# Attention gradients on one core: the query-major exponentials 384 wide with a quarter taken by DMA transposes, and the gradient score matmuls of a half-step on both sides of its burst

## The chip, the core and the metric

The kernel runs on one core of a Trainium2 chip. Time is device time in microseconds (us), from runs of the whole program. One execution was also taken by the hardware profiler; the profile names the engines PE (TensorE matmuls), PEld (TensorE weight loads), DVE (VectorE), ACT (ScalarE), POOL (GpSimd) and SP (SyncE, which only issues DMAs here). The granted TensorE clock (PEclk) is given in shares of full speed.

## The reference

Two branches over the same input are mixed by a gate, and the program returns the output and the gradients of twelve inputs. Cut to what matters here:

```python
x = A_x                                            # 1 x 2048 x 576, bfloat16
g = sigmoid((x * gate_w).sum(-1, keepdims=True))
# branch A: attention, 32 heads of 18
q, k, v = split(x @ wqkv)
p = softmax(einsum("bhqd,bhkd->bhqk", q, k) * 18 ** -0.5)
a = einsum("bhqk,bhkd->bhqd", p, v) ... @ wo
# branch B: a long convolution whose kernel is a sum of complex exponentials
P = exp(logdA[:, :, None] * l)                     # 576 x 128 x 2048
K = einsum("dn,dnl,dn->dl", Cc, P, dB).real
b = irfft(rfft(x) * rfft(K)) + x * Dskip
out = g * a + (1 - g) * b
grads = vjp(out, grad_out)    # of x, wqkv, wo, the seven parameters of B, gate_w
```

The change lies in the gradient of branch A: for every head, the 2048 x 2048 exponentials, dV = P^T dO, dP = dO V^T, dS = P * dP, and dQ, dK from dS.

## The kernel before

The program has three stretches: projections (to about 125 us), the attention loop with its gradients (to about 2105 us), and the convolution branch with the last weight gradients (to the end).

**The attention loop.** Heads go in 8 groups of 4; a *unit* is one group with one block of 512 queries (32 units). The keys come in 16 tiles of 128. Each unit's forward pass is 32 *half-steps*, each for one key tile and one pair of heads; its gradient pass takes 32 half-steps too and runs `OFF` = 39 half-steps behind, so that in nearly every iteration of `for G in range(...)` (L1289) a forward half-step of one unit and a gradient half-step of the unit before it stand side by side. The schedule is written out by hand: instructions go to each engine's queue in program order. One iteration, in PE's order:

- `P1`: two score matmuls K·Q^T, keys on the partitions, one head each, into a PSUM tile `S` (2 buffers). ACT's exponential of it (L1388) gives a `PT` tile (128 keys x 2 heads x 512 queries, bfloat16), from which the forward output and dS are made. `PT` tiles go round in 41 buffers.
- a *burst*, by the slot of the iteration in a round of 8: half of dV (`dv_half`), half of dQ (`dq_half`), half of dK (`dk_half`), or PE transposes of dS (`turn`, tile `turn_p`).
- `P3`: two score matmuls again, but with the *queries* on the partitions (128 queries x 2 heads x 512 keys), into the other `S` buffer. ACT's exponential of it (L1393) gives an `eb` tile, which only `dv_half` reads.
- `P2`: two matmuls dP = V·dO^T (`ps_P2`, two PSUM buffers `dP`), which DVE multiplies by the `PT` tile into `ds` (L1398).
- in half of the iterations, four matmuls of the forward output (`accO`).

DVE first evicts what the burst has finished (`evs`: dvacc L1151, dqa L1169, dkacc L1188, or the copy of `turn_p` L1102) and then does the two `ds` products. Once a `ds` tile is full, SP issues a DMA transpose of it into `dsT` (L1406) for `dk_half`, some 6 to 9 half-steps before that reads it. SP also loads K, Q, V strips and transposes finished gradients into `gT` (L1071); its queue is one list, in order.

**Beside it on POOL.** `e_emit` (end of each iteration, left out in the first two of a unit) puts the elementwise work of branch B's exponential basis into POOL's queue, some in every iteration (L506, stored by L559), and `pack` puts the re-packing of finished gradients there (L1075, L1076). Once per unit, two half-steps after its last `accO`, `post_forward` runs: PE turns the output, DVE takes the reciprocal `rl` (L1044), **POOL** makes `dOa` (L1049) and `prod` (L1051) from it, and in the next iteration DVE reduces `prod` (L1057, in `f2`); two iterations later PE turns `dOa` into `dOaT`, which all of that unit's `P2` need. POOL's queue is in order as well: `dOa` stands behind all basis work put there before it.

Of the kernel before, what the change touches and what calls it, by code (L numbers as in the profile page):

```python
# [10 lines left out]
ACT = mybir.ActivationFunctionType  # L11
BF = mybir.dt.bfloat16
# [5 lines left out]
P = 128  # L18


def build(tc, aps, dbg_aps=None, stages=("s1", "attn", "post", "s4", "final")):
# [7 lines left out]
    def mm(out, lhsT, rhs, start=True, stop=True, **kw):  # L29
        return nc.tensor.matmul(out, lhsT=lhsT, rhs=rhs, start=start, stop=stop, **kw)  # L30
# [31 lines left out]
    with ExitStack() as gctx:  # L62
# [63 lines left out]
        woT = [eds.tile([P, 2, 512], BF, tag="eb", bufs=8, name="eb").rearrange("p a b -> p (a b)")[:, 0:D] for _ in range(DC)]  # L126
        dO_st = [eds.tile([P, 2, 512], BF, tag="eb", bufs=8, name="eb") for _ in range(3)]
# [822 lines left out]
        if "attn" in stages:  # L950
            KB = 512
            NQ = S // KB
            TPQ = KB // P
            DA = HP
            NFILL = {"V": 1, "Q": 0, "K": 0}
            with ExitStack() as ctx:
                ctx.enter_context(tc.manual_schedule(engines={mybir.EngineType.PE, mybir.EngineType.Activation, mybir.EngineType.DVE, mybir.EngineType.Pool, mybir.EngineType.SP}))
# [130 lines left out]
                def by_pe(p):  # L1088

                    return {NPF: 0, NPF + 1: 1}.get(p, 2)  # L1090
# [15 lines left out]
                def ds_tiles(U, p):  # L1106

                    n = by_pe(p)
                    return [U["ds"][2 * p + 2 - n + x][:, 3, :] for x in range(n)], [(n, lambda: U["dsT", p][:, 2 - n:2, 3 * TPQ:, :])]

                def do_tile(U):
                    U["dOaT"] = work.tile([P, TPQ, P], BF, tag="dOaT", name="dOaT")
                    return [U["dOa"].rearrange("p t a b -> p (t a b)")], [(1, lambda: U["dOaT"].unsqueeze(1))]
# [175 lines left out]
                for G in range(NTOT + OFF + 24):  # L1289
# [18 lines left out]
                    if r1:  # L1308
                        g, b, i, j0 = r1
                        T = grp_t[g]  # L1310
                        ps = s_pair("P1")
                        for x in range(2):
                            row(ps[:, x, :], T["KaT", i // TPQ][:, (i % TPQ) * P:(i % TPQ + 1) * P], T["QaT", b], j0 + x)
                        rows.append(("P1", g, b, i, j0, ps))
                    evs = []
                    slot = (G2 + 1) % 8
                    m_ = (G2 - (7, 8, 8, 8, 8, 8, 8, 0)[slot]) // 8
# [28 lines left out]
                    if r2:  # L1346
                        g, b, s2 = r2
                        T = grp_t[g]
                        U = UN[(g, b)]
                        par_ = (s2 + OFF) % 2  # L1350
                        jo = 2 * par_
                        kq, ii = s2 // 8, (s2 % 8) // 2
                        ps = s_pair("P3")
                        for x in range(2):
                            row(ps[:, x, :], T["QaT", b][:, ii * P:(ii + 1) * P], T["KaT", kq], jo + x)
                        rows.append(("P3", g, b, (kq, ii), jo, ps))
                        i2 = s2 // 2
                        for x in range(2):
                            j2 = 2 * (1 - par_) + x
                            ps = apsp.tile([P, KB], F32, tag="dP", bufs=2, name="ps_P2")  # L1360
                            row(ps, T["VaT", i2 // TPQ][:, (i2 % TPQ) * P:(i2 % TPQ + 1) * P], U["dOaT"].rearrange("p t q -> p (t q)"), j2)
                            rows.append(("P2", g, b, i2, j2, ps))
# [16 lines left out]
                    if 1 <= G <= 2 * NT:  # L1379
                        do_half(G - 1)  # L1380

                    for e_ in evs:
                        e_()
                    for (kind, g, b, i, j, ps) in rows:
                        U = UN[(g, b)]
                        if kind == "P1":
                            U["PT"][i, j // 2] = pt_tile()
                            nc.scalar.activation(U["PT"][i, j // 2], ps, ACT.Exp)  # L1388
                        elif kind == "P3":
                            e = eds.tile([P, 2, KB], BF, tag="eb", bufs=8, name="eb")  # L1390
                            for x in range(2):
                                U["eb"][(i[0], i[1], j + x)] = e[:, x, :]
                            nc.scalar.activation(e, ps, ACT.Exp)  # L1393
                        else:
                            if i not in U["ds"]:
                                U["ds"][i] = eds.tile([P, 4, KB], BF, tag="ds", bufs=5, name="ds")
                                U["dsn", i] = 0
                            nc.vector.tensor_tensor(U["ds"][i][:, j, :], ps, U["PT"][i, j // 2][:, j % 2, :], op=A.mult)  # L1398
                            U["dsn", i] += 1
                            nj = 3 if by_pe(i // 2) >= 2 - i % 2 else 4  # L1400
                            if U["dsn", i] == nj:
                                p = i // 2
                                assert j == nj - 1
                                if i % 2 == 0:
                                    U["dsT", p] = work.tile([P, 2, 4 * TPQ, P], BF, tag="dsT", bufs=3, name="dsT")
                                nc.sync.dma_start_transpose(out=U["dsT", p][:, i % 2, 0:nj * TPQ, :],  # L1406
                                                            in_=U["ds"][i][:, 0:nj, :].rearrange("p j q -> p (j q)"))
# [467 lines left out]
```

## Time and profile before

| | |
|---|---|
| median of 3 runs | 2677.37 us (2671.75 to 2682.45) |
| span of the profiled execution, first to last instruction | 2673.6 us |
| PE, DVE, ACT, POOL busy, whole span | 2405.5, 2294.7, 2352.0, 1830.1 us |
| ACT exponentials `PT` and `eb` | 1024 each, 1075 and 1070 ns |
| DVE products `ds` | 2048, 683 ns |
| DMA transposes `dsT<-ds` | 512 |

The page has no time of its own for the profiled execution beside its span; the median is 3.8 us above that span, and two of the three runs are above it. In the page a row of a group reads: line, engine, operation, out<-in, shapes, count, busy time and mean, and then the idle time of the engine just before, with what ended it. Instructions of one engine overlap in their pipelines, so their durations can add up to more than the time between their starts.

### The profile page before, as it was taken

What the parts mean: (1) busy time and instruction counts of PE and PEld (TensorE: products, weight loads), DVE (VectorE), ACT (ScalarE), POOL (GpSimd) and SP (SyncE); (2) the same over time, 40 slices, a digit from 0 to 9 for tenths busy, and PEclk for the clock granted to TensorE, in tenths of its full rate; (3) what the DMA queues carried; (4) which work ended last, traced back from release to release, by engine and by line L of the source; (5) the groups of instructions that cost most, each with busy time, mean ns of one, the idle gap of its engine ahead of it and who ended that gap; (6) DMA issues with size and microseconds to landing.
All of it is one profiled execution on the core that took longest, in us unless ns stands there. A gap on an engine that the chain in (4) does not pass through costs nothing.

```text
span 2673.6 us, 69952 instructions
## 1 busy us (share of the span) xinstructions
PE 2405.5 (90%) x27411; PEld 1134.6 (42%) x27411; DVE 2294.7 (86%) x4090; ACT 2352.0 (88%) x2744; POOL 1830.1 (68%) x2845
## 2 busy tenths in 40 slices
PE   8999999998889898889898999989988699999999
PEld 4433333333333333333333333333232489998756
DVE  5748999999889999889899999999897499999964
ACT  5589999999999999999999999999996489999321
POOL 0388878888888888888878888887931135555431
PEclk9989999999999999999999999999896699999999
DMA  7747889879979978997898899779668979998996
GB/s 232 202 114 152 150 171 177 162 156 181 169 151 172 185 157 163 173 167 152 165 179 157 157 172 169 154 164 181 134 136 174 224 229 262 260 263 250 269 255 136
DMA packets 1155478, 486.63 MB, mean 182 GB/s; under 512 B 1071062, under 2 KB 1108551, under 8 KB 1152843
## 3 DMA queue, kind: packets, MB, share of 16 engines
q1 hardware_dynamic: 1108346, 339.13, 64.3%
q0 software_dynamic: 44784, 137.52, 19.2%
q10 hardware_dynamic: 2016, 5.51, 0.7%
q8 instruction: 214, 3.51, 0.6%
q14 instruction: 118, 0.96, 0.1%
HBM read 146.27 MB, written 93.80 MB: 90 GB/s over the span
## 4 chain that ended last, share of the span: by engine, by line
ACT 39%; PE 28%; DVE 22%; issue 6%; DMA 3%; POOL 2%; SPq 1%; ACTq 0%; DVEq 0%; POOLq 0%
ACT eb L1393 23%; ACT PT L1388 14%; PE ps_P L30 8%; DVE ds L1398 7%; DVE tz L733 3%; DVE wab L753 3%; PE accV L30 2%; PE ps_dx L30 2%; PE turn_p L1097 2%; DVE tz L736 2%; PE accK L30 2%; DVE HG L738 2%; PE yp L30 2%; DVE Rw L758 1%; DVE dvacc L1151 1%
## 5 line engine op out<-in xcount | busy, mean ns | idle before, releaser
L1398 DVE TENSOR_TENSOR ds<-ps_P,PT 128x512 bf16<-128x512 f32 x2048 | 1312.5, 683 | 127.8 <-PE ps_P L30 87.3
L1393 ACT ACTIVATE eb<-ps_P 128x1024 bf16<-128x1024 f32 x1024 | 1095.7, 1070 | 44.3 <-PE ps_P L30 44.2
L1388 ACT ACTIVATE PT<-ps_P 128x1024 bf16<-128x1024 f32 x1024 | 1099.6, 1075 | 11.0 <-PE ps_P L30 9.5
L30 PE MATMUL ps_P<-dOaT,VaT_g 32*128 32x512 bf16 x2048 | 583.1, 390 | 30.8 <-DVE ds L1398 15.4
L506 POOL TENSOR_TENSOR et<-eG,eT 128x448 f32<-128x448 f32 x576 | 542.9, 963 | 10.7
L30 PE MATMUL ps_P<-QaT_g,KaT_g 32*128 32x512 bf16 x2048 | 404.7, 387 | 126.6 <-ACT PT L1388 122.2
L30 PE MATMUL ps_P<-KaT_g,QaT_g 32*128 32x512 bf16 x2048 | 408.9, 392 | 2.0 <-ACT eb L1393 1.4
L506 POOL TENSOR_TENSOR Eo<-et,et 128x448 bf16<-128x448 f32 x288 | 327.2, 1136 | 20.8
L30 PEld LDWEIGHTS <-KaT_g 32*128 32x128 bf16 x2048 | 147.4, 91 | 456.1 <-issue 438.2
L30 PEld LDWEIGHTS <-QaT_g 32*128 32x128 bf16 x2048 | 115.7, 91 | 288.6 <-issue 266.7
L30 PE MATMUL accV<-eb,dOa 128*32 128x512 bf16 x2048 | 185.6, 396 | 26.8 <-ACT eb L1393 26.5
L30 PE MATMUL accO<-PT,Vtok_g 128*32 128x512 bf16 x2048 | 207.9, 395 | 0.1
L30 PE MATMUL accK<-dsT,Qtok_g 128*32 128x256 bf16 x4096 | 165.3, 283 | 21.3 <-DMA dsT<-ds 19.9
L30 PE MATMUL accQ<-ds,Ktok_g 128*32 128x512 bf16 x2048 | 161.9, 394 | 2.2 <-DVE dvacc L1151 1.9
L30 PEld LDWEIGHTS <-Vtok_g 128*32 128x32 bf16 x2048 | 52.8, 93 | 222.6 <-issue 222.6
L1102 DVE COPY dsT<-turn_p 128x1024 bf16<-128x1024 bf16 (+1 forms) x216 | 139.2, 644 | 3.4 <-PE turn_p L1097 3.4
L1097 PE MATMUL turn_p<-ident_bf,ds 128*128 128x128 bf16 x1664 | 136.2, 225 | 1.4 <-DVE gb L1169 0.8
L672 ACT COPY E1e<-etp 128x1024 bf16<-128x1024 bf16 x132 | 125.4, 1063 | 2.7 <-PE etp L671 2.7
L30 PEld LDWEIGHTS <-Qtok_g 128*32 128x32 bf16 x4096 | 88.6, 97 | 87.8 <-issue 57.9
L506 POOL TENSOR_TENSOR et<-eT 128x32 f32<-128x32 f32 (+3 forms) x288 | 116.2, 424 | 11.4
L1097 PEld LDWEIGHTS <-ds 128*128 128x128 bf16 x1664 | 98.9, 100 | 50.2 <-issue 50.0
L1075 POOL COPY dtk<-gT 128x288 bf16<-128x288 bf16 x96 | 40.9, 426 | 107.6 <-DMA dqkv_d<-dtk 47.2
(295 smaller groups left out, 3731.0 us busy)
## 6 DMA issues: line engine op xcount, KB each, us to landing
E_d<-Eo POOLq DMA_DIRECT2D x144, 256.0 KB, 3.3
E1n<-E_d POOLq DMA_DIRECT2D x30, 1024.0 KB, 6.6
T0w<-Kp_d SPq DMA_DIRECT2D x18, 1024.0 KB
xs<-xb_d POOLq DMA_DIRECT2D x28, 512.0 KB, 9.9
dsT<-ds SPq DMA_TRANSPOSE x512
dqkv_d<-dtk POOLq DMA_DIRECT2D x96, 72.0 KB, 4.3
Md_d<-mst SPq DMA_DIRECT2D x18, 288.0 KB
skw<-Md_d SPq DMA_DIRECT2D x72, 64.0 KB
```

What stands on the lines that cost most here:

```text
L30: return nc.tensor.matmul(out, lhsT=lhsT, rhs=rhs, start=start, stop=stop, **kw)
L506: nc.gpsimd.tensor_tensor(out, a, b, op=op)
L672: copy(E_[:, 4 * q:4 * q + 4], pt_)
L733: nc.vector.tensor_tensor(tz[x], HG[:, :, k - 1].unsqueeze(1).to_broadcast([P, 2, 2, n, CB]), ZZ.unsqueeze(3).to_broadcast([P, 2, 2, n, CB ...
L736: nc.vector.tensor_tensor(tz[x][:, 0], tz[x][:, 0], UVk[:, :, :, k, :], op=A.add)
L738: nc.vector.tensor_tensor(HG[:, :, k], tz[x][:, 0], tz[x][:, 1, ::-1], op=A.add)
L753: nc.vector.tensor_tensor(wab, h_, w_, op=A.mult)
L1097: nc.tensor.transpose(pt_[:, x, qb, :], t_[:, qb * P:(qb + 1) * P], ident_bf)
L1102: (nc.scalar.copy if NTOT <= now[0] < NTOT + OFF else nc.vector.tensor_copy)(o_(), pt_[:, x:x + n])
L1388: nc.scalar.activation(U["PT"][i, j // 2], ps, ACT.Exp)
L1393: nc.scalar.activation(e, ps, ACT.Exp)
L1398: nc.vector.tensor_tensor(U["ds"][i][:, j, :], ps, U["PT"][i, j // 2][:, j % 2, :], op=A.mult)
```

## The change

1. `P3` scores and the exponentials `eb` are made for the first 384 of each 512 keys only (`KT = KB - P`): the ACT instruction works on 128 x 768 instead of 128 x 1024, the two matmuls on 384 columns.
2. The last 128 keys of each block of 512 come from the key-major `PT` tile that the forward pass has made: for each unit and each block, two DMA transposes (`turn_p`, one for each pair of heads, 128 x 1024 each) bring `PT` tile `4 kq + 3` into a new tile `PTt` (2 buffers). They stand in SP's queue at the head of gradient half-steps `8 kq + 1` and `8 kq + 2`; `dv_half` reads them at `8 kq + 7` and `8 kq + 8`.
3. `dv_half` issues, for each 128 queries, four matmuls of 384 columns on `eb` and four of 128 columns on `PTt`, where it had four of 512; the order is stored, turned, turned, stored.
4. Of the two `P2` matmuls of a half-step the first now stands between `P1` and the burst, the second stays behind `P3`. DVE's evictions `evs`, which stood ahead of both `ds` products, stand between them.

```diff
+            KT = KB - P
+            TURNED = (0, 1)
...
+                def turn_p(u, kq, pair):
+                    U = UN[u]
+                    t_ = U["PTt", kq, pair] = work.tile([P, 2 * TPQ, P], BF, tag="PTt", bufs=2, name="PTt")
+                    nc.sync.dma_start_transpose(out=t_, in_=U["PT"][kq * TPQ + 3, pair].rearrange("p x q -> p (x q)"))
...
                 def dv_half(g, b, kq, h, acc):
                     U = UN[(g, b)]
-                    for ii in (2 * h, 2 * h + 1):
+                    def stored(ii):
                         for j in range(4):
-                            mm(acc[HP * j:HP * (j + 1), :], lhsT=U["dOa"][:, ii, j, :], rhs=U["eb"].pop((kq, ii, j)),
+                            mm(acc[HP * j:HP * (j + 1), 0:KT], lhsT=U["dOa"][:, ii, j, :], rhs=U["eb"].pop((kq, ii, j)),
                                start=(ii == 0), stop=(ii == 3), tile_position=(0, HP * j))
+                    def turned(ii):
+                        for j in range(4):
+                            mm(acc[HP * j:HP * (j + 1), KT:KB], lhsT=U["dOa"][:, ii, j, :], rhs=U["PTt", kq, j // 2][:, j % 2 * TPQ + ii, :],
+                               start=False, stop=False, tile_position=(0, HP * j))
+                    stored(2 * h)
+                    turned(2 * h)
+                    turned(2 * h + 1)
+                    stored(2 * h + 1)
...
+                for u_ in range(NU):
+                    for kq_ in range(NQ):
+                        for x_, pair_ in enumerate(TURNED):
+                            at(("pre", u_ * NST + OFF + 8 * kq_ + 1 + x_), lambda u_=u_, kq_=kq_, pair_=pair_: turn_p(units[u_], kq_, pair_))
...
                         rows.append(("P1", g, b, i, j0, ps))
+                    def p2(x):
+                        g, b, s2 = r2
+                        i2, j2 = s2 // 2, 2 * (1 - (s2 + OFF) % 2) + x
+                        ps = apsp.tile([P, KB], F32, tag="dP", bufs=2, name="ps_P2")
...
+                        rows.append(("P2", g, b, i2, j2, ps))
+                    if r2:
+                        p2(0)
...
                         for x in range(2):
-                            row(ps[:, x, :], T["QaT", b][:, ii * P:(ii + 1) * P], T["KaT", kq], jo + x)
+                            row(ps[:, x, 0:KT], T["QaT", b][:, ii * P:(ii + 1) * P], T["KaT", kq][:, 0:KT], jo + x)
                         rows.append(("P3", g, b, (kq, ii), jo, ps))
-                        for x in range(2):
-                            j2 = 2 * (1 - par_) + x
-                            ps = apsp.tile([P, KB], F32, tag="dP", bufs=2, name="ps_P2")
...
+                        p2(1)
...
-                    for e_ in evs:
-                        e_()
+                    if not r2:
+                        for e_ in evs:
+                            e_()
...
-                            e = eds.tile([P, 2, KB], BF, tag="eb", bufs=8, name="eb")
+                            e = eds.tile([P, 2, KT], BF, tag="eb", bufs=8, name="eb")
...
-                            nc.scalar.activation(e, ps, ACT.Exp)
+                            nc.scalar.activation(e, ps[:, :, 0:KT], ACT.Exp)
...
                             nc.vector.tensor_tensor(U["ds"][i][:, j, :], ps, U["PT"][i, j // 2][:, j % 2, :], op=A.mult)
                             U["dsn", i] += 1
+                            if j % 2 == 0:
+                                for e_ in evs:
+                                    e_()
```

More of the change, by code (lines that the diff above doesn't have):

```diff
@@ L125, in build @@
         d_aT = [eds.tile([P, 4, 512], BF, tag="ds", bufs=5, name="ds") for _ in range(DC)]
-        woT = [eds.tile([P, 2, 512], BF, tag="eb", bufs=8, name="eb").rearrange("p a b -> p (a b)")[:, 0:D] for _ in range(DC)]
-        dO_st = [eds.tile([P, 2, 512], BF, tag="eb", bufs=8, name="eb") for _ in range(3)]
+        woT = [eds.tile([P, 2, 384], BF, tag="eb", bufs=8, name="eb").rearrange("p a b -> p (a b)")[:, 0:D] for _ in range(DC)]
+        dO_st = [eds.tile([P, 2, 384], BF, tag="eb", bufs=8, name="eb") for _ in range(3)]
         with ExitStack() as ctx:
@@ L1314, in build @@
                         rows.append(("P1", g, b, i, j0, ps))
+                    def p2(x):
+                        g, b, s2 = r2
+                        i2, j2 = s2 // 2, 2 * (1 - (s2 + OFF) % 2) + x
+                        ps = apsp.tile([P, KB], F32, tag="dP", bufs=2, name="ps_P2")
+                        row(ps, grp_t[g]["VaT", i2 // TPQ][:, (i2 % TPQ) * P:(i2 % TPQ + 1) * P], UN[(g, b)]["dOaT"].rearrange("p t q -> p (t q)"), j2)
+                        rows.append(("P2", g, b, i2, j2, ps))
+                    if r2:
+                        p2(0)
                     evs = []
@@ L1354, in build @@
                         for x in range(2):
-                            row(ps[:, x, :], T["QaT", b][:, ii * P:(ii + 1) * P], T["KaT", kq], jo + x)
+                            row(ps[:, x, 0:KT], T["QaT", b][:, ii * P:(ii + 1) * P], T["KaT", kq][:, 0:KT], jo + x)
                         rows.append(("P3", g, b, (kq, ii), jo, ps))
-                        i2 = s2 // 2
-                        for x in range(2):
-                            j2 = 2 * (1 - par_) + x
-                            ps = apsp.tile([P, KB], F32, tag="dP", bufs=2, name="ps_P2")
-                            row(ps, T["VaT", i2 // TPQ][:, (i2 % TPQ) * P:(i2 % TPQ + 1) * P], U["dOaT"].rearrange("p t q -> p (t q)"), j2)
-                            rows.append(("P2", g, b, i2, j2, ps))
+                        p2(1)
                     tail = []
```

## The prediction

> **What bounds the kernel now.** I read the busy lines of the page first, then the attention loop alone (200 to 1900 us), then what each engine waits for there, and then the loop in order of time.
>
> ```profile
> PE 2405.5 (90%) x27411; PEld 1134.6 (42%) x27411; DVE 2294.7 (86%) x4090; ACT 2352.0 (88%) x2744; POOL 1830.1 (68%) x2845
> ACT 39%; PE 28%; DVE 22%; issue 6%; DMA 3%; POOL 2%; SPq 1%; ACTq 0%; DVEq 0%; POOLq 0%
> core 0: us, PE busy (x) PEld busy (x) DVE busy (x) ACT busy (x) POOL busy (x), PEclk, DMA share, GB/s
> 200.00:1900.00 1700.00, 1529.42 (x16525) 532.79 (x16521) 1531.45 (x2526) 1691.64 (x1836) 1437.67 (x2345) 0.99 0.87 165
> ```
>
> In the loop ACT is busy 1691.6 of 1700 us. Its 1836 instructions are two for each half-step, so 918 half-steps ran there, 1700/918 = 1.852 us each. Over the whole span POOL looks idle a third of the time, but that share is a mean over stages: in the loop it is 85% busy before its own DMA issues are counted. Waits decide who has room:
>
> ```profile
> PE ps_P L30 <- ACT PT L1388: 112.8, 439, 0.4
> POOL dOa L1049 <- DVE rl L1044: 84.0, 24, 5.1
> POOL E_d L559 <- POOL Eo L506: 39.2, 132, 0.3
> POOL dtk L1075 <- DMA dqkv_d<-dtk: 34.6, 18, 5.6
> POOL dqkv_d L1076 <- POOL dtk L1075: 27.6, 84, 1.0
> DVE dOa L1057 <- POOL prod L1051: 3.2, 2, 1.8
> POOL dtk L1075 <- DMA gT<-dvacc: 2.8, 2, 1.8
> PE accK L30 <- DMA dsT<-ds: 2.1, 2, 1.9
> ```
>
> PE waits for ACT (112.8 us): ACT is the bound. But POOL waits for the loop only 84.0 + 2.8 = 86.8 us in 1700. The rest of its idle time ends by its own work or its own store landing (the columns: us in total, times, longest). So POOL's own work is 1700 - 86.8 = 1613.2 us, or 1613.2/918 = 1.757 us for a half-step, only 5% under today's pace.
>
> **The change, part by part.**
>
> *Exponentials.* The pace of ACT in an undisturbed stretch:
>
> ```profile
> 1005.31 1.02 ACT L1388 ACTIVATE PT<-ps_P 128x1024 bf16<-128x1024 f32 x1
> 1006.21 1.03 ACT L1393 ACTIVATE eb<-ps_P 128x1024 bf16<-128x1024 f32 x1
> 1007.11 1.04 ACT L1388 ACTIVATE PT<-ps_P 128x1024 bf16<-128x1024 f32 x1
> 1004.62 2.67 DVE L1398 TENSOR_TENSOR ds<-ps_P,PT 128x512 bf16<-128x512 f32 x4
> L708 ACT ACTIVATE UV<-uvp 128x512 bf16<-128x512 f32 x144 | 75.6, 619 | 8.8 <-PE uvp L30 8.6
> L849 ACT COPY m<-misc 128x384 f32<-128x384 f32 x18 | 9.0, 500 | 8.2 <-PE misc L30 8.2
> ```
>
> Starts lie 0.90 us apart, so ACT needs 1.81 us for two. No 128x768 row exists: between the 512-wide row (0.62) and 1.02 here an element costs 0.78 ns, between 384 wide (0.50) and 1.02 0.81 ns. 256 elements fewer are 0.20 to 0.21 us; I take 0.21, so ACT could run 1.60 us a half-step. Alone that would be 918 x (1.852 - 1.60) = 231 us. The other engines do not allow it: DVE's busy time is 1531.45/918 = 1.668 us and PE's 1529.42/918 = 1.666, both somewhat too high as demands, since pipelined ends are in them (four `ds` in a row take 2.67/4 = 0.67, alone 0.68). Each of these lies under POOL's 1.757.
>
> *POOL becomes the pacer.* The diff leaves POOL's queue alone, and nothing in that queue waits for a half-step except `dOa`, once per unit. When POOL gets there late, DVE stands at the reduction of `prod`, with both `ds` products of the next half-step, PE's `P2`, and so ACT behind it. The trace shows this:
>
> ```profile
> 699.07 0.25 DVE L1044 RECIPROCAL rl<-accF 128x16 f32<-128x16 f32 x1
> 702.14 0.69 POOL L1049 TENSOR_TENSOR dOa<-dO_b,rl 128x288 bf16<-128x288 bf16 x1
> 703.63 0.46 DVE L1057 TENSOR_REDUCE dOa<-prod 128x16 bf16<-128x288 f32 x1 [1.38 <-POOL prod L1051]
> 704.74 0.38 PE L1097 MATMUL turn_p<-ident_bf,dOa 128*128 128x128 bf16 x4 [1.13 <-DVE dkacc L1183]
> 1887.25 0.46 DVE L1057 TENSOR_REDUCE dOa<-prod 128x16 bf16<-128x288 f32 x1 [1.79 <-POOL prod L1051]
> 1888.35 0.38 PE L1097 MATMUL turn_p<-ident_bf,dOa 128*128 128x128 bf16 x4 [1.53 <-DVE dkacc L1183]
> ```
>
> There `rl` was done at 699.32 and POOL came 2.8 us late. Now it happens twice in 29 units; at 1.67 us a half-step POOL would fall behind (1.757 - 1.67) x 32 = 2.8 us in every unit, so the loop goes at POOL's pace: at most 86.8 us are saved in this stretch. If POOL's waits for its own stores (34.6) shrank too, it would be 121; if they grow, less.
>
> *What a late POOL costs beyond its lateness.*
>
> ```profile
> 703.00:706.00 3.00, 1.65 (x19) 0.84 (x16) 2.37 (x5) 2.21 (x4) 2.92 (x4) 1.00 0.48 78
> 1887.00:1892.00 5.00, 3.65 (x24) 1.05 (x25) 4.11 (x8) 3.13 (x4) 4.84 (x6) 0.67 0.50 105
> 1892.00:1900.00 8.00, 7.87 (x60) 1.53 (x56) 4.88 (x8) 6.04 (x6) 7.37 (x10) 0.50 0.51 102
> 1900.00:1910.00 10.00, 9.81 (x87) 3.71 (x81) 7.65 (x13) 8.41 (x9) 9.13 (x12) 0.54 0.57 137
> ```
>
> After PE had been idle 1.13 us the clock stayed at 1.00; after 1.53 us it fell to 0.50 for some 20 us, in which ACT was idle 23 - 17.6 = 5.4 us. Both late units are ones in which POOL also re-packs the K and V gradients of the group before; seven groups are followed by such a unit. While the clock is down POOL works on, so part of the 5.4 us is not lost; bounds 0 and 5.4 each, I take 3, about the middle: 7 x 3 = 21 us back. On this the Trainium skill, "TensorE: Matmul & The Clock Gate", section "Why this matters for your kernels", has a rule: no PE-idle gaps over about 3 us between matmul bursts, else half clock. By it stalls of 1.5 to 3 us would cost nothing and the 21 us would stay saved; the row at 1887 says otherwise.
>
> *The DMA transposes.* 256 more on SP's queue and the DMA engines (issue times as minimum/median/maximum ns):
>
> ```profile
> L1406 SPq DMA_TRANSPOSE dsT<-ds x512: 1274/1458/5387, 175.8 to 2098.6; - x171
> L1071 SPq DMA_TRANSPOSE gT<-gb x32: 1202/1258/3732, 245.6 to 2103.1; - x32
> q1 hardware_dynamic: 897982, 229.35, 74.5%
> q0 software_dynamic: 18416, 48.27, 12.0%
> GB/s 0 0 0 0 51 212 287 287 289 292 287 292 289 292 289 287 284 297 167 29 3 0 0 0 0 0 0 0 0 0 0 0 0 0 0 0 0 0 8 143
> ```
>
> A 512-wide one takes SP 1.26 us, the 1536- or 2048-wide 1.46; a 1024-wide one lies between, 1.35. Two for each 8 half-steps are 2.7 us, beside 4 x 1.46 for `dsT` and about three other issues of at most 1.26: 12.3 of 8 x 1.757 = 14.1 us. SP fits, without much over. The queue lines are those of 200 to 1900 us; the slices of 1004 to 1008 us (0.1 us each) show one running at 290 GB/s. The busy share of 0.87 therefore overstates: 229.35 + 48.27 = 277.6 MB in 1700 us are 163 GB/s. The new ones are 0.26 MB each, 0.9 us at 290; 230 of them add 60 MB, and 338 MB in some 1640 us are 206 of 290. Hidden, with six half-steps until `dv_half` reads them; uncovered, 256 x 0.9 = 230 us. The Trainium skill, "DMA: Bandwidth & Descriptors", section "Latency and other measured facts", gives DMA transposes 261 GB/s on one kernel, which speaks against the change: about 79% of the limit instead of 71%. The trace's 290 is higher, and the sum is the same.
>
> `turn_p` of the next block waits on SP until `dv_half` has read `PTt`; loads and one `dsT` stand behind it, for at most about one half-step, and `dk_half` needs that `dsT` six or more later: 0.
>
> *PE.* `P3` loses a quarter of its columns (gain, hidden). `dv_half` has 16 matmuls for 8, with the same columns.
>
> ```profile
> 1001.46 0.62 PE L30 MATMUL accV<-eb,dOa 128*32 128x512 bf16 x8
> 1128.19 0.62 PE L30 MATMUL accK<-dsT,Qtok_g 128*32 128x256 bf16 x16
> 1127.66 4.38 SPq L1071 DMA_TRANSPOSE gT<-dvacc  x1
> 1132.01 1.05 PE L30 MATMUL accK<-dsT,Qtok_g 128*32 128x256 bf16 x16 [1.85 <-DMA dsT<-ds]
> 1130.00:1134.00 4.00, 2.15 (x26) 0.82 (x24) 1.50 (x4) 1.86 (x3) 3.58 (x6) 0.61 1.11 183
> 1134.00:1138.00 4.00, 4.00 (x33) 1.42 (x30) 2.95 (x5) 3.39 (x4) 1.93 (x4) 0.53 1.20 204
> ```
>
> `dk_half`, 16 of half the width, takes the same 0.62 us as 8: 0, at most +0.1 for the 128-wide ones (256 x 0.1 = 26 us, hidden behind POOL). The early `P2` gives DVE a product to do while PE does the burst and takes the eviction off its head. Its price: if DVE has not freed the `dP` buffer, PE stops there with the burst, `P3` and ACT's `eb` behind it; between 0 and one eviction (0.68) in the five of eight half-steps that have one. Evictions now delay the second `ds`, and its `dsT`, by 0.6 us: covered by the same six half-steps.
>
> *Outside 200 to 1900.* Some 60 half-steps of the end gain 0.1 us each; the last 60 us, where transposes are waited for, lose about as much: 0.
>
> **Sum:** 2673.6 - 86.8 + 21 = 2608 us of span; with the 3.8 us by which the median stands above it, 2612.
>
> **Rivals.**
> 1. *The clock does not fall* (chance 0.16): stalls come spread over all units, each under the 1.13 us that left the clock alone. 2612 - 21 = 2591; with POOL's own waits gone, 2555. For it: most units are late little. Against it: the units with packs.
> 2. *POOL is no limit* (0.08): its lag is taken up somewhere and DVE's 1.67 paces: 918 x (1.852 - 1.67) = 167, 2677 - 167 = 2510. Against it: the two rows at 703 and 1887.
> 3. *The chain holds* (0.17): the early `P2` stops PE, and half-steps take 1.80: 918 x 0.052 = 48 saved, 21 lost to the clock: 2677 - 27 = 2650.
> 4. *Slower* (0.12): the 256 added transposes make those of `ds` late for `dk_half`. Place: SP's queue where gradients are stored; price: as at 1127, where one 4.38 us issue made PE wait 1.85 us and the clock fell, ACT idle 8 - 5.25 = 2.75 us. Once per unit that is 32 x 2.75 = 88 us: 2700. It decides from about 24 such events, (86.8 - 21)/2.75. For it: DMA shares of 1.11 and 1.20. Against it: 2.1 us of such waits in 1700.
> 5. *No shorter exponential* (0.07): two pieces of 384 cost as much as one of 1024, 2677.
>
> **How the numbers follow.** My forecast has 0.40. The range leaves out rivals 2 and 4: 2555 to 2680; the likeliest case alone spans 2591 to 2640. A change under 0.5% (13 us) cannot be told from none here. Faster: 0.40 + 0.16 + 0.08 + most of rival 3 = 0.78; same: the rest of it and rival 5, 0.10; slower 0.12.
>
> **What would show it.** `eb` rows of about 0.81 to 0.86 us at 128x768; ACT's busy time in the loop near 92%; POOL's wait for `rl` near nothing; DVE's wait for `prod` in most units, summing to tens of us; PEclk under 1 after some. Wrong: POOL still waiting for `rl` by 50 us or more (something else paces), `accV` waiting for `PTt`, or `accK` for `dsT` often.

## The result and the profile after

The changed kernel takes 2718.78 us (median of 4 runs, 2709.34 to 2726.30) where the kernel before takes 2676.62 in the same comparison: a ratio of 1.0151, 95% interval 1.0116 to 1.0187. It is slower by 1.5%. The profiled execution has a span of 2724.3 us.

From the page of the changed kernel: busy times, the granted clock and the DMA share in 40 slices, the shared hardware queue, and the chain that ended last by engine:

```profile
PE 2399.4 (88%) x29459; PEld 1166.6 (43%) x29459; DVE 2283.1 (84%) x4090; ACT 2170.5 (80%) x2744; POOL 1830.5 (67%) x2845
...
PEclk9979987897898898889989988888996699999999
DMA  7659999999999999999999999999999979998995
...
q1 hardware_dynamic: 1378682, 406.27, 81.9%
...
PE 38%; DVE 17%; DMA 14%; ACT 14%; issue 3%; POOL 1%; SPq 1%; ACTq 0%; DVEq 0%; POOLq 0%
```

No engine bounds the loop any more. ACT, the fullest before, fell from 2352.0 to 2170.5 us of work, as it was meant to, but the span grew, so its share is 80%. PEclk, which stood at 9 in nearly all of the loop, moves between 7 and 9. The hardware queue's packets take 81.9% (64.3% before), and transfers are now 14% of the chain (3% before).

The loop alone, 200 to 1900 us (columns: stretch, length, busy time and count of PE, PEld, DVE, ACT and POOL, clock, DMA share, GB/s):

```profile
200.00:1900.00 1700.00, 1480.08 (x17854) 543.93 (x17850) 1479.80 (x2456) 1490.47 (x1787) 1403.39 (x2283) 0.89 1.12 195
```

1787 ACT instructions are 893.5 half-steps, so one takes 1700/893.5 = 1.903 us, against 1.852 before and 1.78 in my sum ((1700 - 86.8 + 21)/918). All four engines are idle for 12 to 17% of it. The clock is 0.89 on the mean. The page's group of the shortened exponentials:

```profile
L1419 ACT ACTIVATE eb<-ps_P 128x768 bf16<-128x768 f32 x1024 | 858.7, 839 | 236.8 <-PE ps_P L30 226.7
```

The exponential of 768 columns takes 839 ns, but ACT is idle 236.8 us before it, nearly all of it until PE has made `ps_P` (44.3 us before the change). PE is late because it waits itself. The chief waits in 200 to 1900 us (total, times, longest):

```profile
ACT eb L1419 <- PE ps_P L30: 171.6, 224, 6.4
POOL dOa L1051 <- DVE rl L1046: 86.9, 22, 7.0
PE accV L30 <- DMA PTt<-PT: 61.9, 42, 4.7
POOL dtk L1077 <- DMA gT<-dvacc: 53.6, 19, 6.6
PE accK L30 <- DMA dsT<-ds: 23.3, 16, 5.3
PEld L30 <- DMA dsT<-ds: 16.6, 18, 5.5
```

PE waits 61.9 us for `PTt` and 23.3 us for `dsT`, 85.2 us together; PEld's 16.6 us for `dsT` lie in large part in the same stretches and can't be added. Before, `dsT` was worth 2.1 us and there was no `PTt`. The gradients' transposes, which stand in the same queue, are late too: POOL waits 53.6 us for `gT`, before 2.8. PE's 85.2 us can't make up ACT's waits of 171.6 alone. Of ACT's 209.5 idle us in this stretch, 60 lie in those waits of PE and 125 in stretches in which the clock is at half (the two overlap in part). How that goes shows in one stretch of the timeline (start, length, instruction, idle time before it and what ended it), first SP's queue, then PE and ACT:

```profile
739.19 1.88 SPq L1435 DMA_TRANSPOSE dsT<-ds  x1
741.17 5.13 SPq L1116 DMA_TRANSPOSE PTt<-PT  x1
746.40 2.62 SPq L1435 DMA_TRANSPOSE dsT<-ds  x1
```

```profile
750.56 0.40 PE L30 MATMUL accV<-PTt,dOa 128*32 128x128 bf16 x6 [4.70 <-DMA PTt<-PT]
...
751.74 0.81 ACT L1419 ACTIVATE eb<-ps_P 128x768 bf16<-128x768 f32 x1 [5.47 <-PE ps_P L30]
```

and the same stretch in windows (columns as above):

```profile
740.00:744.00 4.00, 3.98 (x66) 1.92 (x64) 3.98 (x8) 4.00 (x6) 3.84 (x5) 1.00 0.96 146
744.00:748.00 4.00, 1.45 (x14) 0.37 (x14) 2.30 (x4) 2.28 (x3) 3.60 (x6) 0.98 1.25 146
748.00:752.00 4.00, 1.44 (x16) 0.36 (x15) 0.15 (x1) 0.26 (x1) 2.71 (x3) 0.50 1.03 212
752.00:756.00 4.00, 4.00 (x39) 0.97 (x37) 3.12 (x5) 3.30 (x4) 1.39 (x3) 0.50 1.31 223
756.00:760.00 4.00, 3.84 (x35) 1.23 (x33) 3.00 (x5) 3.14 (x4) 3.62 (x5) 0.74 1.13 192
```

The second transpose of `PTt` for this block holds SP for 5.13 us, where the median is 1.28. PE gets its data only at 750.56, another 4.3 us after that issue has ended and after 4.70 us of waiting; ACT has been idle 5.47 us when the next exponential starts. From 748 to about 758 us the clock is at half, and from 752 to 756 PE is busy 4.00 of 4.00 us while ACT has 3.30: PE bounds there because it is slow. By the stretches of constant clock in the trace 34 such falls begin between 200 and 1900 us, 396 us in sum (2 and 27 us before). Around the start of 26 of the 34 (6 us before to 1.5 us after), PE's longest wait is for `PTt` or `dsT`. Between the falls ACT reaches the pace that I gave it: exponentials `eb` start at 695.61, 697.20 and 698.80 us, 1.59 us apart.

### The profile page after: what moved, and what is told of

The parts are those of the page before. It is cut to its first block, busy times and chain, and to the rows that moved or that the text cites. A ratio compares the mean times of both kernels' runs of the same rounds, so it can differ in the third digit from the quotient of the medians.

```text
span 2724.3 us, 74661 instructions
## 1 busy us (share of the span) xinstructions
PE 2399.4 (88%) x29459; PEld 1166.6 (43%) x29459; DVE 2283.1 (84%) x4090; ACT 2170.5 (80%) x2744; POOL 1830.5 (67%) x2845
## 3 DMA queue, kind: packets, MB, share of 16 engines
q1 hardware_dynamic: 1378682, 406.27, 81.9%
## 4 chain that ended last, share of the span: by engine, by line
PE 38%; DVE 17%; DMA 14%; ACT 14%; issue 3%; POOL 1%; SPq 1%; ACTq 0%; DVEq 0%; POOLq 0%
PE ps_P L30 13%; DMA PTt<-PT 9%; ACT eb L1419 7%; ACT PT L1414 6%; DVE ds L1424 6%; PE accV L30 6%; PE accK L30 4%; DMA dsT<-ds 4%; PE accO L30 4%; PE accQ L30 2%; DVE wab L753 2%; DVE tz L733 2%; PE ps_dx L30 2%; DVE tz L736 1%; DVE HG L738 1%
## 5 line engine op out<-in xcount | busy, mean ns | idle before, releaser
L1414 ACT ACTIVATE PT<-ps_P 128x1024 bf16<-128x1024 f32 x1024 | 1080.6, 1056 | 49.0 <-PE ps_P L30 48.2
L1419 ACT ACTIVATE eb<-ps_P 128x768 bf16<-128x768 f32 x1024 | 858.7, 839 | 236.8 <-PE ps_P L30 226.7
L30 PE MATMUL ps_P<-dOaT,VaT_g 32*128 32x512 bf16 x2048 | 825.9, 423 | 4.8 <-DVE ds L1424 4.8
L30 PE MATMUL ps_P<-QaT_g,KaT_g 32*128 32x512 bf16 x2048 | 463.2, 417 | 99.2 <-ACT PT L1414 95.1
L30 PE MATMUL ps_P<-KaT_g,QaT_g 32*128 32x384 bf16 x2048 | 374.0, 362 | 1.2 <-ACT PT L1414 0.5
L30 PE MATMUL accV<-eb,dOa 128*32 128x384 bf16 x2048 | 196.0, 374 | 17.1 <-ACT eb L1419 10.0
L30 PEld LDWEIGHTS <-dOa 128*32 128x32 bf16 x4096 | 88.7, 101 | 235.8 <-issue 226.7
L30 PE MATMUL accQ<-ds,Ktok_g 128*32 128x512 bf16 x2048 | 183.5, 440 | 1.0 <-DVE dvacc L1168 1.0
L30 PEld LDWEIGHTS <-VaT_g 32*128 32x128 bf16 x2048 | 180.3, 92 | 2.4 <-issue 2.4
L30 PE MATMUL accV<-PTt,dOa 128*32 128x128 bf16 x2048 | 93.6, 240 | 72.1 <-DMA PTt<-PT 71.5
```

Of the source, the lines that this page charges most:

```text
L1419: nc.scalar.activation(e, ps[:, :, 0:KT], ACT.Exp)
```

## The experiments

My theory after reading this (T): the 256 added transposes are what costs; they load SP's queue and the DMA engines, PE waits, and the clock falls. The rival (R): the new order of the matmuls, or the 128-wide ones, slow PE.

**Without the transposes.** The matmuls that read `PTt` read constant tiles.

```diff
-  t_ = U["PTt", kq, pair] = work.tile(..., tag="PTt", bufs=2, ...)
-  nc.sync.dma_start_transpose(out=t_, in_=U["PT"][kq * TPQ + 3, pair]...)
+  U["PTt", kq, pair] = ptc[pair]     # set to 1.0 once
```

> The changed kernel without its 256 DMA transposes of PT: the matmuls that read PTt read two constant tiles instead (so a quarter of dV's terms are left out of the output). All else is as in the changed kernel: exponentials 384 wide, 16 matmuls in dv_half, the gradient scores on both sides of the burst. Theory T (the transposes are what costs: they lengthen the shared queue, PE waits for PTt and dsT, and the granted clock falls each time): 2590 to 2630 us, granted clock back to 0.95 or more, PE's waits for dsT under 10 us in 200 to 1900 us, SP's share of time spent on issues back to about 0.66. Theory R (the order of the matmuls or the narrow matmuls of dv_half are what costs): 2690 us or more, clock still about 0.90. My forecast's step that POOL becomes the pacer: POOL's waits for rl near nothing, DVE waiting for prod in most units, units of 32 half-steps at 55 us or a little more.

Measured 2589.16 us, ratio to before 0.9662 (0.9632 to 0.9691). The loop's row and its waits:

```profile
200.00:1900.00 1700.00, 1512.91 (x19295) 579.30 (x19293) 1587.86 (x2653) 1593.06 (x1930) 1494.30 (x2434) 0.95 0.94 173
```

```profile
ACT eb L1423 <- PE ps_P L30: 83.8, 119, 4.4
DVE dOa L1059 <- POOL prod L1053: 29.0, 17, 3.8
PE accK L30 <- DMA dsT<-ds: 14.2, 9, 2.7
POOL dOa L1051 <- DVE rl L1046: 7.4, 6, 2.3
```

The transposes cost 2718.8 - 2589.2 = 130 us, and everything else in the change together gains 2676.0 - 2589.2 = 87. R has fallen. Two signs that I had set for T were missed: PE still waits 14.2 us for `dsT` (I had put under 10), and SP spends 72% of the time on issues (I had put 66). The rest of my forecast holds here: POOL waits 7.4 us for `rl` (84.0 before), DVE waits for POOL's `prod` 17 times, and a half-step takes 1700/965 = 1.762 us, where I had put POOL's pace at 1.757. The units (32 half-steps; here and below from the start of one unit's first exponential `PT` to the next's) take 53.5 to 59.8 us from the third on. One late unit shows the chain of the forecast, POOL to DVE to PE to ACT:

```profile
1075.65 0.46 DVE L1059 TENSOR_REDUCE dOa<-prod 128x16 bf16<-128x288 f32 x1 [3.77 <-POOL prod L1053]
1076.75 0.57 PE L30 MATMUL ps_P<-dOaT,VaT_g 32*128 32x512 bf16 x1 [3.45 <-DVE ds L1428]
1078.89 0.81 ACT L1423 ACTIVATE eb<-ps_P 128x768 bf16<-128x768 f32 x1 [4.41 <-PE ps_P L30]
```

The clock fell to half at 1076.8 us, for 6.8 us.

**The order alone.** Before's kernel with only the second part of the change: 512-wide exponentials, no `PTt`.

```diff
+  if r2:
+      p2(0)          # first ps_P2 row ahead of the burst
   ...
-  row(ps, ...); rows.append(("P2", ...))   # both rows behind P3
+  p2(1)
```

> The kernel before with the second part of the change alone: the first ps_P2 matmul row stands ahead of the burst, the evictions between the two ds products. Exponentials 512 wide, no transposes of PT, dv_half with 8 matmuls. Theory T (transposes cost): 2650 to 2680 us, the clock 0.96 or more, ACT still the fullest engine with its 1.85 us for each half-step. Theory R (the order costs): 2700 us or more, with ACT's wait for PE's ps_P at 100 us or more in 200 to 1900 us and PE waiting for DVE's ds before ps_P2.

Measured 2678.96 us against 2675.98, ratio 1.0017 (0.9997 to 1.0037): no effect to be seen, the clock at 0.99 in the loop. The price of the early `P2`, which I had bounded by 0 and 0.68 us a half-step, is 0 at this kernel's pace, where ACT is the bound.

**Transposes that nobody reads.** All 256 are issued, the narrow matmuls read `eb`.

```diff
-  rhs=U["PTt", kq, j // 2][:, j % 2 * TPQ + ii, :]
+  rhs=U["eb"][(kq, ii, j)][:, 0:P]
```

> The changed kernel with all its DMA transposes of PT still issued, at the same places of SP's order, but with nobody reading PTt: the 128-wide matmuls of dv_half read columns 0 to 127 of eb instead (so a quarter of dV's terms is wrong). It takes away one wait, that of PE for PTt (61.9 us in 200 to 1900 us after the change, 42 times), and leaves the load on SP and on the DMA engines. Theory T1 (PTt's own lateness costs): 2600 to 2640 us, clock 0.95 or more. Theory T2 (the load costs: dsT's transposes behind them come late, too): 2680 to 2720 us, clock 0.90 to 0.93, PE's and PEld's waits for dsT at 40 us or more. Theory R (order or narrow matmuls): 2700 us or more, with waits for dsT about as now.

Measured 2700.51 us, ratio 1.0087 (1.0057 to 1.0117). Taking the wait for `PTt` away, PE's and with it SP's for a free `PTt` buffer, gains 18 us of the 130 (each time is known to about 8 to 10 us). The other 111 are load:

```profile
ACT eb L1419 <- PE ps_P L30: 165.6, 170, 7.4
PE accK L30 <- DMA dsT<-ds: 98.6, 39, 7.0
PEld L30 <- DMA dsT<-ds: 63.7, 39, 5.2
```

With `PTt`'s wait gone, PE waits 98.6 us for `dsT`, and PEld 63.7, mostly at the same times: the next thing in the same queue is late instead.

**POOL's large stores.** In the changed kernel's trace the packets of one store of `E_d` (256 KB) span 0.7 us at the least and 2.1 us at the median; before, the median is 1.3. So theory T3: stores and transposes slow each other. A square of two by two, with seven of eight stores left out, with and without the transposes. The later loads of `E_d` then read the row that was stored.

```diff
-  nc.gpsimd.dma_start(E_d[:, q // EQ, ...], Eo.pop(q)...)
+  e_ = Eo.pop(q)
+  if q // EQ % 8 == 0:
+      nc.gpsimd.dma_start(E_d[:, q // EQ, ...], e_...)
```

> The changed kernel with seven of eight of POOL's stores E_d<-Eo (256 KB each) left out; the later loads of E_d read the row that was stored instead, so the outputs that depend on E_d are wrong. All 256 transposes stay. With the transposes left out instead the time was 2589 us, with nobody reading them 2700. Theory T3 (transposes and POOL's large stores slow each other on the DMA engines): 2600 to 2650 us, SP's issues of dsT back to a median of 1.5 us, clock 0.94 or more. Theory T4 (SP's queue is full by the issues themselves, whatever the engines do): 2680 to 2720 us, SP's share of issue time still over 0.88.

> Neither the 256 transposes (constant tiles in place of PTt) nor seven of eight of POOL's E_d stores: the fourth corner of a square with the changed kernel (2719 us), the one without transposes (2589) and the one with fewer stores. Left out are a quarter of dV's terms and most of E_d. If the stores cost by what they do to the transposes alone (T3), this lies near 2580; if POOL's own time is what paces the kernel without transposes, POOL is relieved here of its store issues and of its waits for Eo (41 us in 200 to 1900 us) and it lies at 2520 to 2570 us with the units at 52 to 54 us.

Measured 2649.81 us (0.991, 0.9876 to 0.9944) with the transposes and 2535.70 (0.9492, 0.9443 to 0.9541) without. The first lies just inside T3's range, while the clock in the loop, 0.92, stays under T3's 0.94 and SP's share of 89% is as T4 has it. SP's issues of `dsT` are nearly as short as T3 said, although all 256 added transposes are issued (minimum, median and maximum ns):

```profile
L1437 SPq DMA_TRANSPOSE dsT<-ds x512: 1274/1565/5370, 178.3 to 2068.9; - x171
```

The median is 1.76 us in the changed kernel, so the stores have a share in the stretching. In the time that share is small: fewer stores gain 69 and 53 us, and the transposes cost 114 us with fewer stores and 130 with all. The difference, 16 us, is less than the four intervals (8 to 13 us each way) can tell from none: T3 as the main cause has fallen. What fewer stores do besides is relieve POOL, as the loop of the kernel without either shows (to 1850 us, since it ends earlier):

```profile
200.00:1850.00 1650.00, 1477.04 (x19392) 578.44 (x19395) 1591.57 (x2665) 1595.48 (x1939) 1424.48 (x2319) 0.98 0.88 159
```

```profile
POOL dOa L1053 <- DVE rl L1048: 73.3, 27, 6.4
DVE dOa L1061 <- POOL prod L1055: 1.4, 1, 1.4
```

DVE waits for POOL's `prod` once instead of 17 times, POOL waits 73.3 us for `rl` again, and a half-step takes 1650/969.5 = 1.702 us. That fits POOL as the one that set the pace in the kernel without transposes.

**Issue or data.** The kernel with unread transposes, once with each of the 256 narrowed to 128 columns (the issue stays, an eighth of the data), once with each replaced by a plain copy of the same 256 KB.

```diff
-  nc.sync.dma_start_transpose(out=t_, in_=U["PT"][kq * TPQ + 3, pair]...)
+  nc.sync.dma_start_transpose(out=t_[:, 0, :], in_=U["PT"][...][:, 0, 0:P])   # narrow
+  nc.sync.dma_start(t_..., U["PT"][kq * TPQ + 3, pair]...)                    # plain copy
```

> The kernel in which nobody reads PTt (2700 us), with each of the 256 added transposes 128 columns wide in place of 1024: the same number of issues at the same places of SP's queue, an eighth of the bytes and packets for the DMA engines. Theory T4 (SP's in-order issue time is what costs; by the rows 512 wide takes 1.22 us to issue and 1024 wide 1.29, so a narrow one should take at least 1.1): 2670 to 2700 us, PE's and PEld's waits for dsT still 80 us or more, SP's share 0.88 or more. Theory T5 (the DMA engines' load is what costs): 2590 to 2620 us, waits for dsT under 20 us, SP's share about 0.82.

> The kernel in which nobody reads PTt (2700 us), with each of the 256 added transposes replaced by a plain DMA copy of the same 256 KB from SBUF to SBUF: the same bytes in 2 KB rows in place of 256-byte packets, and an issue of about 0.57 us by the rows of plain loads in place of 1.29. Theory T4 (issue time): 0.7 us x 256 = 184 us less of SP, its share between those of the kernels with one and with no transposed pair (0.82 and 0.72): 2600 to 2640 us. Theory T5 in bytes (the engines have no room for 67 MB more): 2670 to 2700 us. Theory T5 in packets (256-byte packets are what loads the engines): 2590 to 2620 us, as without the transposes.

Measured 2618.70 us (0.9798, 0.9776 to 0.9820) and 2605.69 us (0.9735, 0.9704 to 0.9765). Of the 111 us of load, the narrow transposes leave 30 and the plain copies 17. The narrow ones' time lies in the range of T5 (the engines' load), but SP's share of 89% and PE's waits of 61 us for `dsT` don't fit T5; the plain copies' time rules out bytes and lies in the ranges of both T4 (issue time) and T5 in packets. So neither theory alone fits all signs: issues alone cost little, bytes alone cost little; what costs is full transposes. The loops of the kernel with unread transposes and of the one with plain copies:

```profile
200.00:1900.00 1700.00, 1445.09 (x17962) 544.00 (x17961) 1490.42 (x2469) 1491.73 (x1797) 1409.39 (x2295) 0.90 1.13 197
```

```profile
200.00:1900.00 1700.00, 1489.52 (x19129) 568.89 (x19128) 1581.66 (x2631) 1580.64 (x1913) 1495.69 (x2435) 0.95 1.07 208
```

SP's rows for `dsT` and `PTt`, of the changed kernel, of the one without the added transposes (`dsT` alone), of the narrow and of the plain one:

```profile
L1435 SPq DMA_TRANSPOSE dsT<-ds x512: 1285/1758/5470, 184.4 to 2148.0; - x171
```

```profile
L1116 SPq DMA_TRANSPOSE PTt<-PT x256: 1231/1282/5135, 180.5 to 2132.6; - x128
```

```profile
L1439 SPq DMA_TRANSPOSE dsT<-ds x512: 1273/1560/5467, 178.6 to 2007.2; - x171
```

```profile
L1435 SPq DMA_TRANSPOSE dsT<-ds x512: 1274/1544/5565, 178.9 to 2037.1; - x171
```

```profile
L1116 SPq DMA_TRANSPOSE PTt<-PT x256: 1121/1184/2551, 174.0 to 2021.7; - x128
```

```profile
L1116 SPq DMA_DIRECT2D PTt<-PT x256: 477/541/2676, 178.2 to 2013.4; - x128
```

A transpose of 128 columns takes SP 1.18 us to issue, one of 1024 columns 1.28: the issue hardly depends on the size. But the `dsT` behind it does: its median is 1.46 us before, 1.56 at the faster pace without `PTt`, 1.54 behind narrow ones and 1.76 behind full ones. With more transposes and stores under way SP's issues take longer; by what mechanism no run here shows. Summed over 300 to 1900 us of the timeline, SP spends 66% of the time on issues before, 72% without the transposes, 84% with plain copies, 89% with narrow ones, 92% in the changed kernel and 94% with unread ones.

The units tell where the load costs. Every fourth unit, in which a group changes, takes 58.4 us on the mean without the transposes, 64.3 with plain copies, 65.9 with narrow transposes and 70.4 with full ones that nobody reads. The unit just before each of these takes 55.0, 54.9, 55.6 and 59.9; the other two of four lie between 53.8 and 57.5 in all four kernels. With any of the three additions SP has 41 issues in the fourth unit, 35 to 36 in the one before and 31 to 32 in the others. So the 111 us fall nearly all into the units where SP has most to issue, and in the fullest of them even cheap issues cost something.

The Trainium skill, "Advanced Engine Details and Errata", section "X-Bar Transpose (TRN2)", says that transposing DMAs are as fast as regular ones. It speaks of the transfer's speed; as a load on this kernel the two are not alike: the same 67 MB cost 17 us as plain copies and 111 us as transposes.

**One pair.** Only pair 0 turned, 128 transposes; `eb` 384 wide for pair 0 and 512 for pair 1 (four buffers each), one `PTt` buffer, all outputs in full.

```diff
-  KT = KB - P
-  TURNED = (0, 1)
+  KT = (KB - P, KB)     # by pair
+  TURNED = (0,)
```

> The changed kernel with half of its transposes: only head pair 0 has its quarter from PTt (128 transposes, exponentials 384 wide for pair 0 and 512 wide for pair 1, 8 + 8 narrow matmuls in dv_half's place of 16 + 8); one PTt buffer. All outputs are computed in full. ACT's floor for a half-step is about 1.725 us on the mean of the two (1.852 - 0.21/2 lies at 1.75). Theory T with a threshold (SP and the engines have room for one more transpose in 8 half-steps, not for two): 2600 to 2640 us, clock 0.95 or more. Theory T in proportion (each transpose costs its share): 2640 to 2700 us, clock 0.92 to 0.95. Theory R (order or narrow matmuls): 2690 us or more.

Measured 2635.54 us, ratio 0.9846 (0.9806 to 0.9886). It lies in the range of the threshold, near its end, and its units say why. Most take 55.9 us; every fourth takes 63.4 on the mean (60 to 67). Two neighbours in windows:

```profile
1041.50:1097.30 55.80, 48.30 (x608) 19.51 (x608) 53.16 (x88) 55.60 (x65) 50.61 (x81) 1.00 1.08 190
```

```profile
1097.30:1164.40 67.10, 54.11 (x608) 20.73 (x608) 54.13 (x89) 56.72 (x65) 49.31 (x80) 0.87 1.04 186
```

The second is a unit at a group's end: beside the usual issues SP has nine of the sixteen that a change of group brings (four transposes of K and V gradients, five loads of the next group). SP's timeline from within it:

```profile
1112.31 2.10 SPq L1435 DMA_TRANSPOSE dsT<-ds  x1
1114.52 3.72 SPq L1116 DMA_TRANSPOSE PTt<-PT  x1
1118.33 2.47 SPq L1435 DMA_TRANSPOSE dsT<-ds  x1
1120.89 1.22 SPq L1073 DMA_TRANSPOSE gT<-dvacc  x1
1122.16 1.29 SPq L1012 DMA_TRANSPOSE Ktok_g<-QKV_d  x1
1123.54 1.49 SPq L1435 DMA_TRANSPOSE dsT<-ds  x1
```

These follow each other without a gap of more than 0.12 us; three of the six are `dsT`, each behind another transfer. In the changed kernel SP's issues of such a unit sum to 62 us and it takes 67.6; in the other three kinds they sum to 50 to 58 us and these take 56 to 62. A unit of the kernel without transposes has 35 to 49 us of issues and takes 55 to 58. So in the changed kernel, where SP has 50 us or more to issue in a unit, the unit's time goes with it, 4 to 6 us above (about 0.1 us lies between two issues, and there are 31 to 40 of them). That is a reading of sums side by side; the next runs test it.

**The crowded units.** Two ways to relieve them. First, the eight gradient stores issued 24 half-steps later, with one pair and with both turned.

```diff
-  at(("pre", G + 2), lambda ...: store_grad(DKV.pop(...), ...))
+  at(("pre", G + 2 + (24 if g + 1 < NG else 0)), lambda ...: store_grad(DKV.pop(...), ...))
```

> The kernel with one pair turned (2636 us), with the issue of the transposes that store the K and V gradients of a finished group (gT<-dvacc, gT<-dkacc, 8 for each of the first seven groups) moved 24 half-steps later. In that kernel every fourth unit, in which these eight and the next group's K and V loads stand in SP's queue, takes 63.4 us on the mean and the others 55.9. All outputs are computed in full. Theory Q (in those units SP's queue holds more than fits in a unit; spread out, it fits): these units come to 56 to 59 us and the time to 2595 to 2615 us. Rival (the loads or the re-packing themselves cost, wherever they stand): the time stays at 2630 to 2640 us, the same 7 us a group moved to the next unit.

> The changed kernel (2719 us, both pairs turned) with the same shift of the K and V gradients' transposes by 24 half-steps. All outputs are computed in full. There every fourth unit takes 67.6 us, the others 62.1, 58.8 and 56.4. Theory Q says that only the excess of the fourth units can go: 7 times up to 8 us, so 2660 to 2690 us. Theory T5 in packets (transposes need more of the engines than is left, in every unit) says that the work only moves: 2700 to 2720 us.

Measured 2625.42 us with one pair (0.9814, 0.9788 to 0.9839) and 2711.61 with both (1.0137, 1.0092 to 1.0182). The first missed its range: the fourth units fell from 63.4 to 57.5 us, but the ones after them rose from 56.0 to 60.8. Moving the issues by 24 half-steps mostly moved the crowd. With both pairs nothing that can be told from no change came of it, as the second expectation has it: there every unit is nearly full.

Second, one pair, but in the last unit of a group three or two of the four blocks aren't turned; ACT makes their quarter with an exponential of its own.

```diff
+  if j == 0 and not turned_by_dma((g, b), i[0]):
+      ...
+      nc.scalar.activation(U["PTt", i[0], 0]...[:, :, i[1], :], ps[:, :, KT[0]:KB], ACT.Exp)
```

> The kernel with one pair turned (2636 us), but in the last unit of each of the first seven groups, whose backward part runs while SP's queue also holds the gradient stores and the next group's loads, three of the four blocks are not turned: ACT computes their quarter itself with a second exponential of 256 columns (by 839 ns for 768 columns and 1070 for 1024 this is an estimated 0.38 us, 84 of them). All outputs are computed in full. Theory Q (the excess of the fourth units, 63.4 against 55.9 us, is SP's crowded queue): about 5 us of SP and its stretching go in these units, ACT gains 4.6 us of work in them; they come to 58 to 60 us and the time to 2600 to 2620 us. Rival (the excess belongs to the group change itself): the units stay at 63 us or get longer by ACT's work, 2630 to 2660 us.

> As the kernel with three blocks left unturned in those units, with two (the second and the fourth) instead. All outputs are computed in full. Theory Q: half-way, the units at 58 to 61 us and 2600 to 2625 us, ACT having 1.5 us less to do in each than with three. Rival: 2630 to 2655 us.

Measured 2617.23 us (0.9783, 0.9755 to 0.9811) and 2617.58 (0.9779, 0.9754 to 0.9805), inside the ranges of theory Q. The fourth units come to 58.6 and 59.2 us. Whether three or two blocks are left out makes no difference that these runs can tell. The first kernel's added exponentials, and its loop:

```profile
L1429 ACT ACTIVATE PTt<-ps_P x84: 378/433/538, 361.4 to 1779.5; 128x256 bf16<-128x256 f32 x84
```

```profile
200.00:1900.00 1700.00, 1441.97 (x17979) 583.01 (x17978) 1587.26 (x2605) 1673.02 (x1978) 1480.26 (x2417) 0.99 1.00 185
```

ACT pays 0.43 us for each (my estimate was 0.38), and the clock is back at 0.99. Both versions compute everything and beat the kernel before by 2.2% and, by the two ratios, the changed one by 3.6%.

## Why the prediction was wrong

The step that failed is "The DMA transposes": I priced them at 0, "hidden", and they cost 130 us. Three readings in it were wrong.

- *Issue times were taken as constants.* I filled 8 half-steps with 4 x 1.46 us for `dsT` and 2 x 1.35 for `PTt`. `PTt`'s 1.28 us was about right. But the median `dsT` rose to 1.76 us and its mean (300 to 1900 us) from 1.73 to 2.02, so my 12.3 of 14.1 us (87%) became 92%, in half-steps that were themselves longer. Nor was the rest free: about 0.1 us lies between two issues, some nine times in 8 half-steps.
- *The mean over units hid the crowded ones.* "SP fits, without much over" is true of the average and false of every fourth unit, where a group changes and 40 issues stand in place of 31 to 37 (changed kernel, on the mean).
- *The room in GB/s was no room.* I called the DMA share of 0.87 an overstatement, because 206 of 290 GB/s left room. The copies show that GB/s is the wrong measure: the kernel with plain copies moves 208 GB/s in the loop and is 95 us faster than the one with unread transposes, which moves 197. The share alone doesn't tell the cost either: it is 1.12 in the changed kernel and 1.13 with unread transposes, but 1.07 with the plain copies, which cost 17 us.

"Six half-steps until `dv_half` reads them" was no cover either: the lateness isn't that of one transfer but of a queue that never empties. And with that cover gone the cost is not the wait alone: PE's 85.2 us of waits for `PTt` and `dsT` came with 396 us at half clock.

The other steps:

- *The exponential.* Right: 839 ns in the range of 0.81 to 0.86 given, and undisturbed half-steps do run at 1.595 us, the 1.60 of the sum.
- *POOL as the pacer.* Right where the transposes are gone: 1.762 us a half-step where I had 1.757, and the gain of 87 us (known to about 8) is near the 86.8 of the sum. In the changed kernel itself POOL is not the pacer: 86.9 us of waits for `rl`, and 42 waits of `accV` for `PTt`, both of which I had named as signs of being wrong.
- *Early `P2`.* Right in the kernel before: 0, by the order alone. At the faster pace it wasn't measured by itself.
- *`turn_p` waiting on SP for its buffer, 0.* Small: with nobody reading `PTt` this wait is gone together with PE's own for `PTt`, and both are worth 18 us.
- *The 16 matmuls of `dv_half`.* Not measured by themselves; the kernel without transposes has them and comes out at POOL's pace, so they are hidden there.
- *Clock falls, 7 of 3 us each.* Mis-sized, and their price open. The kernel without transposes has 28 of them in the loop, shorter ones (174 us in sum). Around 11 of them (6 us before to 1.5 us after) PE's longest wait is for DVE's `ds`, as in the late unit above, and around 5 for `dsT`; around the other 12 the trace shows no wait of PE over 0.4 us, so the 1.13 us that left the clock alone in one place are no safe bound. And yet the time is 2589 us: rival 1's 2591, whose condition (no falls) didn't hold, and not the 2612 of the sum. That would fit a POOL that works on while the clock is down, as the prediction says in part; that the numbers meet so closely is luck as far as the runs show.

Rival 4 was the mechanism: transposes late for `dk_half`, the clock down after, 2700 us. It named the gradient stores as the place and 2.75 us once per unit as the price (88 us). The place holds for about half, and `PTt` itself was late as well. Of the 130 us some 64 fall into the seven units where a group's K and V gradients are stored (67.6 us against 58.4 without the transposes), and some 50 into the seven just before them (62.1 against 55.0). That rival 4's 2700 lies near the measured 2719 is in part luck: its 88 us were 32 equal events, and the cost is not spread like that.

What stays open is how far the load acts by SP's issues being held and how far by the engines' own throughput. Narrow transposes (30 us) and plain copies (17 us) don't add up to full ones (111 us), which fits one queue near saturation but doesn't split the two. Issuing the transposes from another engine's queue wasn't tried.

## What to carry to other kernels

Work moved off a full engine onto a queue that serves others in order is not free because the queue has room on average: add up its issues in its most crowded unit, with the durations that they have when others are in flight, and ask who reads what stands behind. Here half of the offload, left out where the queue is crowded, gained 2.2%; all of it lost 1.5%. Room in GB/s says little: plain copies of the same bytes cost 17 us.

## What the runs showed of the hardware

- An SP issue of a DMA transpose takes about as long for 128 columns (1.18 us) as for 1024 (1.28 us), and the same issue takes longer with more under way: the median `dsT` takes 1.46 us before and 1.76 us with 256 more transposes, 1.57 with these but an eighth of POOL's large stores, and over 5 us singly in all of them.
- 67 MB more of transposed data (256 of 256 KB) cost this kernel 111 us where plain copies of the same bytes cost 17 us.
- 85 us of PE's waits for transposes, spread over the loop in the changed kernel, went with 396 us at half clock.
